# Keys laid out column by column: the spread of block-diagonal operands in an attention and FFN kernel

## The chip, the core and the metric

The kernel runs on one core of one Trainium2 chip. Its time is the device time of one execution in microseconds. The engines are TensorE (PE, with its weight loads as PEld), VectorE (DVE), ScalarE (ACT), GpSimd (POOL) and SyncE (SP), which issues most of the DMAs.

## The reference

Two things are computed one after the other: a linear attention with a decaying state, over 4 batches, 8 heads, 768 tokens and head dimension 48, and on its output a feed-forward net with a maximum over three products.

```python
def _attn_ref(r, k, v, w, u):
    state = np.zeros((B, H, D, D))
    for t in range(S):
        kt, vt, rt = (k[:, :, t], v[:, :, t], r[:, :, t])
        cur = np.einsum('bhd,bhe->bhde', u[None] * kt, vt)
        y[:, :, t] = np.einsum('bhd,bhde->bhe', rt, state + cur)
        state = w[None, :, :, None] * state + np.einsum('bhd,bhe->bhde', kt, vt)

def _moe_ref(x, w1, w2, w3, w_out):        # x: 3072 x 384, hidden 768
    h = np.maximum(np.maximum(x @ w1, x @ w2), x @ w3)
    return h @ w_out
```

All inputs and the output are float32.

## The kernel before, in words

The 768 tokens are cut into 12 chunks c of 64 tokens. In a chunk the attention is matrix products: scores of 64 by 64 tokens (keys against receptances), masked, times the values, plus the receptances times the state of the chunks before; and the state's update, keys times values. The 32 pairs of batch and head are 16 units of two heads each, and a chunk is worked in two halves q of 8 units (U = 8). The two heads of a unit share one 128 x 128 weight array: one head's 64 rows and columns stand in the upper left block, the other's in the lower right, and the rest is zero. So a product of a unit is one matmul with a block-diagonal weight operand.

To keep the precision, a float32 operand is split into two float16 parts, high and low (`high` on ScalarE, L334; `low` on VectorE, L339 and L341), and a product is three matmuls (`three`, L411): high x high, high x low, low x high. So scores are 24 matmuls a half chunk (weights `kb`, 64 columns moving), keys for the state 24 (weights `ktb`, 48 columns moving), values 48 (weights `vb` and `sb`). The FFN (L489) runs in fp32r with the same three parts and 256 moving columns, 216 matmuls a chunk.

A block-diagonal operand is a `Block` (L308): 128 partitions and, one after the other, two parts s of 8 units of w columns; for the keys w is 128, so a partition holds 2 x 8 x 128 float16 values, 4 KB. ScalarE and VectorE write a dense tile of the same shape (`kd`, `ktd`): all 128 partitions, columns 0 to 63 of each unit (0 to 47 for ktd), zeros behind. Two DMAs (`spread`, L320) carry it into the block-diagonal one (`kb`, `ktb`): partitions 0 to 63 as they stand, with their zeros, and partitions 64 to 127 shifted by 64 columns. Each of kb, ktb, kd and ktd exists once and is used for both halves of every chunk. The weights of a matmul are a slice of 128 neighbouring columns (`on`).

Chunk 0 has no spread. ScalarE writes float32 values straight into the two diagonal blocks (`apart`, L478), in the same bytes seen as 8 units of float32 columns (`wide`), and one full-precision product a unit follows (`full`, L484), for scores, values and keys.

The order of the work is made ahead by a planner (`Plan`, L38): each step has an engine, a due time, a cost and the steps that it needs, the planner plays them through, and the result is the program order of every engine, fixed when the kernel is built. `before_scores` (L718) lines up the scaling of k, `high` and `low` into kd, the spread to kb; `before_keys` (L740) the same for the state's keys; `scored` and `keyed` the matmuls. Each spread is planned as two DMA issues on SP's queue. At the start 16 half weights of the FFN arrive as float64 words and are converted on ScalarE and VectorE (L241 to L252), while chunk 0's attention runs; from c = 3 on GpSimd takes over a part of VectorE's multiplications.

Of the kernel before, what the change touches and what calls it, by code (L numbers as in the profile page):

```python
# [7 lines left out]
F32 = mybir.dt.float32  # L8
F32R = mybir.dt.float32r
F16 = mybir.dt.float16  # L10
# [8 lines left out]
P = 128  # L19
B, H, S, D = 4, 8, 768, 48  # L20
C = 64
# [5 lines left out]
U = 8  # L27
# [10 lines left out]
class Plan:  # L38
# [26 lines left out]
    def do(self, due, eng, cost, fn, reads=(), writes=(), takes=(), size=0, near=0):  # L65


        n = len(self.todo)
        new = [t for _, t in takes]
        made = (*new, *writes, *reads)[0]  # L70
        kind = eng + " " + (made if isinstance(made, str) else made[0])
        late = due > self.OPENING
        due += self.SHIFT.get(kind, (0, 0))[late]
        need = {self.wrote[k] for k in (*reads, *writes) if k in self.wrote}
        for k in writes:
            need |= self.read.get(k, set())
# [74 lines left out]
def kernel(ctx, tc, feat, tok, wu, ut, ws, wo, cst, out):  # L151
    nc = tc.nc
    const = ctx.enter_context(tc.tile_pool(name="const", bufs=1))
    raw = ctx.enter_context(tc.tile_pool(name="raw", bufs=3))
    bd = ctx.enter_context(tc.tile_pool(name="bd", bufs=1))
# [8 lines left out]
    psa = ctx.enter_context(tc.tile_pool(name="psa", bufs=4, space=PSUM))  # L164
# [7 lines left out]
    raws = {}  # L172
# [102 lines left out]
    for g in range(NP):  # L275
        nc.vector.tensor_tensor_scan(
            out=pw[:, g, 1:C + 1], data0=w_sb[:, g:g + 1].broadcast_to([P, C]), data1=ones,
# [27 lines left out]

    class Block:  # L308


        def __init__(self, name, w):
            n = 2 * U * w
            t = bd.tile([P, n + P - w], F16, name=name)
            nc.gpsimd.memset(t.bitcast(F32), 0.0)
            self.flat, self.w = t[:, 0:n], w
            self.dense = self.flat.rearrange("p (s u n) -> p s u n", s=2, u=U)
            self.on = [[t[:, (s * U + i) * w:(s * U + i) * w + P] for i in range(U)] for s in range(2)]
            self.wide = self.flat.bitcast(F32).rearrange("p (u n) -> p u n", u=U)

    def spread(eng, dst, src, by):  # L320
        eng.dma_start(out=dst.flat[0:C], in_=src.flat[0:C])
        eng.dma_start(out=dst.flat[C:P, by:], in_=src.flat[C:P, 0:2 * U * src.w - by])

    kb = Block("kb", P)
    vb = [Block(f"vb{q}", 2 * D) for q in range(2)]
    ktb = Block("ktb", P)
    kd = Block("kd", P)
    vd = [Block(f"vd{q}", 2 * D) for q in range(2)]
    sd = Block("sd", 2 * D)
    sb = [Block(f"sb{q}", 2 * D) for q in range(2)]  # L330
    ktd = Block("ktd", P)

    def high(dense, src, w, scale=1.0):
        nc.scalar.mul(out=dense.dense[:, 0, :, 0:w], in_=src, mul=scale)  # L334

    def low(dense, src, w, scale=1.0):

        if scale == 1.0:
            nc.vector.tensor_tensor(out=dense.dense[:, 1, :, 0:w], in0=src, in1=dense.dense[:, 0, :, 0:w], op=ALU.subtract)  # L339
        else:  # L340
            nc.vector.scalar_tensor_tensor(out=dense.dense[:, 1, :, 0:w], in0=src, scalar=scale, in1=dense.dense[:, 0, :, 0:w], op0=ALU.mult, op1=ALU.subtract)  # L341
# [10 lines left out]

    def units(a):
        return a.rearrange("p g b n -> p (g b) n")

    HS = (slice(0, C), slice(C, P))

    def by_token(a, q):
        return a[:, 2 * q:2 * q + 2].unsqueeze(2).broadcast_to([P, 2, B, D])
# [5 lines left out]
    def scale(c, q, n):  # L365
        t = raws[c, q]
        tb = (wkt if n == "kT" else wrt)[:, 2 * q:2 * q + 2].unsqueeze(2).broadcast_to([P, 2, B, C])
        helper(c).tensor_tensor(out=t[n], in0=t[n], in1=tb, op=ALU.mult)  # L368

    def r_high(c, q):  # L370
        t = raws[c, q]
        t["rh"] = work.tile([P, U, C], F16, name="rh", bufs=2)
        nc.scalar.copy(out=t["rh"], in_=units(t["rT"]))

    def r_low(c, q):
        t = raws[c, q]
        t["rl"] = work.tile([P, U, C], F16, name="rl", bufs=2)
        nc.vector.tensor_tensor(out=t["rl"], in0=units(t["rT"]), in1=t["rh"], op=ALU.subtract)
# [26 lines left out]
    def decay(c, q):  # L405
        t = raws[c, q]
        helper(c).tensor_tensor(out=t["k"], in0=t["k"], in1=by_token(tkt, q), op=ALU.mult)
# [67 lines left out]
    def apart(dst, src, by, scale=1.0):  # L475

        for hh in range(2):
            nc.scalar.mul(out=dst.wide[HS[hh], :, hh * by:hh * by + src.shape[2]], in_=src[HS[hh]], mul=scale)  # L478

    def full(name, q, block, n, w, src):  # L480
        t = raws[0, q]
        ps = t[name] = psa.tile([P, U, n], F32, name="psa")
        for i in range(U):
            nc.tensor.matmul(out=ps[0:w, i, :], lhsT=block.wide[:, i, 0:w], rhs=src[:, i, :], start=True, stop=True)  # L484


    def pairs3(ps, prods, first=True, last=True):
# [89 lines left out]
    def general():  # L577
# [28 lines left out]
        with tc.For_i(0, NCH, 1) as c:  # L606
# [5 lines left out]
            for s in range(C):  # L612
                vr = xp.tile([P, NP, B, D], F32, name="xl")
                for hh in range(2):
                    row = tok[bass.ds(c, 1), :, hh * C + s:hh * C + s + 1, 2].rearrange("c q p g b e -> (c p) q g b e")
                    nc.sync.dma_start(out=vr[HS[hh]].rearrange("p (q g) b e -> p q g b e", q=2), in_=row.broadcast_to([C, 2, 2, B, D]))
                kc, rc = (t[:, :, :, s:s + 1].broadcast_to([P, NP, B, D]) for t in cols)
# [53 lines left out]
    do = plan.do  # L671
# [3 lines left out]
    def dma(due, fn, size, reads=(), writes=(), takes=(), eng="sp", n=1):  # L675
        do(due, eng, n * Plan.ISSUE[eng], fn, reads, writes, takes, size)

    def helping(c, columns):
        return ("pool", 0.05 + 2.5e-3 * columns) if c > 2 else ("dve", dve(columns))

    def dve(columns):
        return 0.07 + 1.05e-3 * columns

    def act(columns):
        return 0.11 + 0.83e-3 * columns
# [32 lines left out]
    def before_scores(c, q, due):  # L718

        h, cost = helping(c, U * C)  # L720
        f, t, u = ("feat", c, q), ("tok", c, q), units
        do(due - 0.32, h, cost, lambda: scale(c, q, "kT"), reads=[f], writes=[("kT", c, q)], near=0.55)
        do(due - 0.30, h, cost, lambda: scale(c, q, "rT"), reads=[f], writes=[("rT", c, q)], near=0.55)
        do(due - 0.26, "act", act(U * C), lambda: high(kd, u(raws[c, q]["kT"]), C), reads=[("kT", c, q)], writes=["kdh"])
        do(due - 0.24, "dve", dve(U * C), lambda: low(kd, u(raws[c, q]["kT"]), C), reads=[("kT", c, q), "kdh"], writes=["kdl"], near=1.2)
        dma(due - 0.22, lambda: spread(nc.sync, kb, kd, C), 524288, reads=["kdh", "kdl"], writes=["kb"], n=2)
        do(due - 0.15, "act", act(U * C), lambda: r_high(c, q), reads=[f, ("rT", c, q)], takes=[("rh", ("rh", c, q))])
        do(due - 0.13, "dve", dve(U * C), lambda: r_low(c, q), reads=[f, ("rT", c, q), ("rh", c, q)], takes=[("rl", ("rl", c, q))], near=1.2)
        before_mask(c, q, due)
# [10 lines left out]
    def before_keys(c, q, due):  # L740
        t = ("tok", c, q)
        h, cost = helping(c, U * D)
        do(due - 0.30, h, cost, lambda: decay(c, q), reads=[t, "tkt"], writes=[("kdec", c, q)], near=0.55)
        do(due - 0.24, "act", act(U * D), lambda: high(ktd, units(raws[c, q]["k"]), D), reads=[t, ("kdec", c, q)], writes=["ktdh"])
        do(due - 0.23, "dve", dve(U * D), lambda: low(ktd, units(raws[c, q]["k"]), D), reads=[t, ("kdec", c, q), "ktdh"], writes=["ktdl"], near=1.2)
        dma(due - 0.20, lambda: spread(nc.sync, ktb, ktd, C), 524288, reads=["ktdh", "ktdl"], writes=["ktb"], n=2)

    def before_values(c, q, due):
        t, vh, vl = ("tok", c, q), ("vdh", q), ("vdl", q)
# [19 lines left out]
    def first_keys(q, due):  # L769
        c, t = 0, ("tok", 0, q)  # L770
        do(due - 0.30, "dve", dve(U * D), lambda: decay(c, q), reads=[t, "tkt"], writes=[("kdec", c, q)], near=0.55)
        do(due - 0.24, "act", 1.05, lambda: apart(ktb, units(raws[c, q]["k"]), C), reads=[t, ("kdec", c, q)], writes=["ktb"])
        do(due, "pe", 3.2, lambda: full("ke", q, ktb, D, C + D, units(raws[c, q]["v"])), reads=["ktb", t], takes=[("psa", ("ke", c, q))])
        after_keys(c, q, due)

    def scored(c, q, due):
# [115 lines left out]
    for q in range(2):  # L892
        first_keys(q, 0.1 + 0.2 * q)
        spread_state(0, q, 0.2 + 0.2 * q)
# [82 lines left out]
```

## Time and profile before

| what | value |
|---|---|
| median of two runs | 417.5 us (415.71 and 419.3) |
| profiled execution | 417.51 us, span 415.6 us, granted clock 0.998 |
| TensorE busy | 392.5 us (94%), 4758 matmuls seen |
| VectorE, ScalarE, GpSimd busy | 285.2, 256.5, 182.4 us |
| moved by DMA | 90.08 MB, mean 217 GB/s |
| weights from kb, from ktb | 528 and 480 half-precision matmuls |
| spreads of kd, of ktd | 22 and 20, two issues each |

In the rows quoted below, `L411 PE MATMUL psa<-rh,kb 128*128 128x64 f16 x352 | 19.2, 193` means: line 411, on TensorE, writes psa from rh and kb, weights of 128 rows and columns, 64 columns moving, 352 times, busy 19.2 us, 193 ns for one. The duration of a matmul or weight load runs from its start to its modelled end; matmuls overlap, so the distance from one start to the next is much shorter than this. Behind the second bar stands the time that the engine was idle just before, with what ended it. In windows each engine has its busy time and in brackets its count.

### The profile page before, as it was taken

Reading aid. Unit: us, or ns where it says so; the run is one execution under the profiler, and the core shown is the slowest. Engines: PE = TensorE matmul, PEld = TensorE weight load, DVE = VectorE, ACT = ScalarE, POOL = GpSimd, SP = SyncE. Lnnn points to the kernel's source line nnn. Section 1 sums busy time; section 2 is a strip of 40 time slices with the busy share of each in tenths; the row PEclk is TensorE's granted clock in tenths of the full one; section 3 lists DMA queues with packets and bytes.
Section 4 is the critical chain, followed back from the end, with each engine's and each line's share of the span. In section 5 each row is a group of like instructions: output and inputs, shape, how many; then the busy total and the mean of one; then the engine's idle time right before and its main releaser. Section 6 shows DMA issues by size and latency. Waiting matters only on the chain.

```text
span 415.6 us, 11976 instructions
## 1 busy us (share of the span) xinstructions
PE 392.5 (94%) x4758; PEld 388.0 (93%) x4758; DVE 285.2 (69%) x551; ACT 256.5 (62%) x674; POOL 182.4 (44%) x180
## 2 busy tenths in 40 slices
PE   1878899999999999999999999999999999999996
PEld 0767899999999999999999999999999999999996
DVE  7798999989597776676576676576676596354240
ACT  2999977796666666466366466366366377265331
POOL 9000000088669664564654754664654551020120
PEclk9999999999999999999999999999999999999999
DMA  7789898789799896876876876876876995886101
GB/s 284 288 269 249 249 278 313 193 244 302 202 270 263 227 250 170 250 196 153 259 192 143 271 194 156 256 196 153 257 192 155 299 322 139 248 289 217 38 2 41
DMA packets 30954, 90.08 MB, mean 217 GB/s; under 512 B 4784, under 2 KB 9648, under 8 KB 30896
## 3 DMA queue, kind: packets, MB, share of 16 engines
q1 hardware_dynamic: 25568, 84.47, 70.7%
q10 hardware_dynamic: 5328, 4.82, 3.7%
q8 instruction: 38, 0.62, 0.6%
q14 instruction: 20, 0.16, 0.1%
HBM read 45.85 MB, written 4.72 MB: 122 GB/s over the span
## 4 chain that ended last, share of the span: by engine, by line
PE 72%; ACT 12%; DVE 6%; DMA 5%; issue 3%; SPq 0%; ACTq 0%; DVEq 0%
PE psm L489 60%; PE psa L411 11%; ACT junk L351 3%; DMA tok<-in_tok_dram 2%; DMA ktb<-ktd 2%; ACT ztop L241 2%; ACT am L399 1%; DVE wl L252 1%; ACT wh L248 1%; DVE m L504 1%; ACT xh L467 1%; DMA out_dram<-io 1%; DVE sc L281 1%; ACT kb L478 1%; DVE raw L245 1%
## 5 line engine op out<-in xcount | busy, mean ns | idle before, releaser
L489 PE MATMUL psm<-xh,wh 128*128 128x256 f32 x648 | 166.3, 286 | 5.0 <-ACT xh L467 2.9
L489 PE MATMUL psm<-xl,wh 128*128 128x256 f32 x648 | 163.4, 282 | 1.1 <-DVE xl L472 1.1
L489 PEld LDWEIGHTS psm<-xh,wh 128*128 128x128 f32 x648 | 123.2, 190 | 5.7 <-ACT xh L467 3.1
L489 PEld LDWEIGHTS psm<-xl,wh 128*128 128x128 f32 x648 | 122.8, 190 | 1.4 <-DVE xl L472 1.4
L489 PE MATMUL psm<-xh,wl 128*128 128x256 f32 x648 | 112.6, 283 | 0.0
L504 DVE TENSOR_TENSOR m<-psm,m 128x256 f32<-128x256 f32 x144 | 60.4, 420 | 64.7 <-PE psm L489 59.1
L489 PEld LDWEIGHTS psm<-xh,wl 128*128 128x128 f32 x648 | 92.8, 190 | 0.0
L368 POOL TENSOR_TENSOR feat<-feat,wrt 128x512 f32<-128x512 f32 x36 | 47.0, 1317 | 76.1 <-DMA feat<-in_feat_dram 75.3
L513 POOL TENSOR_TENSOR hl<-m,hh 128x256 fp32r<-128x256 f32 x55 | 45.4, 827 | 74.5 <-ACT hh L507 74.4
L507 ACT CAST hh<-m 128x256 fp32r<-128x256 f32 x72 | 28.7, 403 | 55.7 <-DVE m L504 55.2
L489 PE MATMUL psm<-hh,woh 128*128 128x256 f32 x216 | 54.3, 284 | 0.0
L489 PE MATMUL psm<-hh,wl 128*128 128x256 f32 x216 | 53.4, 279 | 0.0
L387 POOL TENSOR_TENSOR am<-tok,u_sb 128x384 f32<-128x384 f32 x18 | 21.0, 1168 | 59.2 <-DVE al L431 59.2
L351 ACT ACTIVATE junk<-tok 128x384 bf16<-128x384 f32 x72 | 37.4, 520 | 14.2 <-DMA tok<-in_tok_dram 12.4
L489 PEld LDWEIGHTS psm<-hh,woh 128*128 128x128 f32 x216 | 40.6, 188 | 0.0
L489 PEld LDWEIGHTS psm<-hh,wl 128*128 128x128 f32 x216 | 40.6, 188 | 0.0
L472 DVE SCALAR_TENSOR_TENSOR xl<-psa,xh 32x256 fp32r<-32x256 f32 (+2 forms) x60 | 28.2, 471 | 14.9 <-ACT xh L467 14.0
L489 PE MATMUL psm<-hl,woh 128*128 128x256 f32 x216 | 35.1, 280 | 0.0
L467 ACT ACTIVATE xh<-psa 32x256 fp32r<-32x256 f32 (+2 forms) x60 | 25.1, 418 | 15.8 <-PE psa L411 14.8
L411 PE MATMUL psa<-ah,vb 128*128 128x64 f16 x352 | 32.9, 194 | 0.0
L411 PE MATMUL psa<-rh,sb 128*128 128x64 f16 x352 | 32.5, 193 | 0.0
L339 DVE TENSOR_TENSOR kd<-feat,kd 128x512 f16<-128x512 f32 x22 | 18.3, 830 | 20.4 <-ACT kd L334 17.3
(99 smaller groups left out, 746.3 us busy)
## 6 DMA issues: line engine op xcount, KB each, us to landing
tok<-in_tok_dram SPq DMA_DIRECT2D x24, 576.0 KB, 6.7
raw<-in_ws_dram SPq DMA_DIRECT2D x24, 576.0 KB, 7.4
feat<-in_feat_dram SPq DMA_DIRECT2D x24, 512.0 KB, 5.2
kb<-kd SPq DMA_DIRECT2D x22, 256.0 KB, 5.7
kb<-kd SPq DMA_DIRECT2D x22, 248.0 KB, 5.8
ktb<-ktd SPq DMA_DIRECT2D x20, 256.0 KB, 3.4
ktb<-ktd SPq DMA_DIRECT2D x20, 248.0 KB, 4.2
raw<-in_wo_dram SPq DMA_DIRECT2D x8, 576.0 KB, 5.6
```

The lines of the kernel that those rows point to most:

```text
L241: nc.scalar.copy(out=ztop[h].bitcast(F16).rearrange("p (n two) -> p n two", two=2)[:, :, 1], in_=halves(raw[:, 1:], 3).bitcast(BF16))
L339: nc.vector.tensor_tensor(out=dense.dense[:, 1, :, 0:w], in0=src, in1=dense.dense[:, 0, :, 0:w], op=ALU.subtract)
L351: nc.scalar.activation(out=junk, in_=src, func=AF.Square, scale=scale, accum_out=stat[:, kind, 2 * c + q:2 * c + q + 1])
L368: helper(c).tensor_tensor(out=t[n], in0=t[n], in1=tb, op=ALU.mult)
L387: helper(c).tensor_tensor(out=w.rearrange("p (g b) d -> p g b d", g=2), in0=t["r"], in1=by_token(u_sb, q), op=ALU.mult)
L411: nc.tensor.matmul(out=ps, lhsT=l[i], rhs=rr[j], start=first and n == 0, stop=last and n == 2)
L467: nc.scalar.mul(out=hi, in_=src, mul=SC_X)
L472: nc.vector.scalar_tensor_tensor(out=lo, in0=src, scalar=SC_X, in1=hi.bitcast(F32), op0=ALU.mult, op1=ALU.subtract)
L489: nc.tensor.matmul(out=ps, lhsT=a, rhs=b, start=first and n == 0, stop=last and n == len(prods) - 1)
L504: nc.vector.tensor_tensor(out=to, in0=ps, in1=m, op=ALU.max)
L507: nc.scalar.copy(out=h[0][:, f, :], in_=m)
L513: lows_by(c, f).tensor_tensor(out=h[1][:, f, :], in0=m, in1=h[0][:, f, :].bitcast(F32), op=ALU.subtract)
```

## The change

Four tiles get a new layout: `kb` and `ktb` become `Planes`, `kd` and `ktd` become `Dense`. In both a partition holds one column after the other, and in a column the 16 float16 values of two parts and eight units, 32 bytes. Neighbouring columns of one unit are thus 32 bytes apart. `Dense` has 64 columns (2 KB a partition), `Planes` 128 (4 KB), of which the off-diagonal blocks are zeroed once at the start. A spread copies two blocks of 64 partitions by 64 columns, 2 KB a partition, still as two DMAs on SP's queue.

The weights of a matmul are now 128 columns with a step of 32 bytes. `high` and `low` write with that step, and `low` reads the high part with it. Chunk 0's float32 copies (`apart`) write 4 bytes in every 32, and its full-precision products read their weights so; the keys' product takes 128 columns instead of 112. The planner's costs, sizes and due times stay the same. `vb`, `sb`, `vd` and `sd` keep their layout.

```diff
+    class Dense:
+        def __init__(self, name):
+            self.t = bd.tile([P, C, 2, U], F16, name=name)
+            nc.gpsimd.memset(self.t.bitcast(F32), 0.0)
+            self.dense = self.t.rearrange("p n s u -> p s u n")
+
+    class Planes:
+        def __init__(self, name):
+            self.t = bd.tile([P, 2 * C, 2 * U], F16, name=name)
+            nc.gpsimd.memset(self.t.bitcast(F32), 0.0)
+            self.on = [[self.t[:, :, s * U + i] for i in range(U)] for s in range(2)]
+            self.wide = self.t.bitcast(F32)
+
+        def place(self, hh, by, n):
+            return self.wide[HS[hh], hh * C:hh * C + n].rearrange("p n u -> p u n")
+
+        def whole(self, i, n):
+            return self.wide[:, :, i]
+
+    def spread_planes(dst, src):
+        for hh in range(2):
+            nc.sync.dma_start(out=dst.t[HS[hh], HS[hh]], in_=src.t[HS[hh]].rearrange("p n s u -> p n (s u)"))
...
-    kb = Block("kb", P)
+    kb = Planes("kb")
...
-    ktb = Block("ktb", P)
-    kd = Block("kd", P)
+    ktb = Planes("ktb")
+    kd = Dense("kd")
...
-    ktd = Block("ktd", P)
+    ktd = Dense("ktd")
...
-            nc.scalar.mul(out=dst.wide[HS[hh], :, hh * by:hh * by + src.shape[2]], in_=src[HS[hh]], mul=scale)
+            nc.scalar.mul(out=dst.place(hh, by, src.shape[2]), in_=src[HS[hh]], mul=scale)
...
-            nc.tensor.matmul(out=ps[0:w, i, :], lhsT=block.wide[:, i, 0:w], rhs=src[:, i, :], start=True, stop=True)
+            nc.tensor.matmul(out=ps[0:w, i, :], lhsT=block.whole(i, w), rhs=src[:, i, :], start=True, stop=True)
...
-        dma(due - 0.22, lambda: spread(nc.sync, kb, kd, C), 524288, reads=["kdh", "kdl"], writes=["kb"], n=2)
+        dma(due - 0.22, lambda: spread_planes(kb, kd), 524288, reads=["kdh", "kdl"], writes=["kb"], n=2)
...
-        dma(due - 0.20, lambda: spread(nc.sync, ktb, ktd, C), 524288, reads=["ktdh", "ktdl"], writes=["ktb"], n=2)
+        dma(due - 0.20, lambda: spread_planes(ktb, ktd), 524288, reads=["ktdh", "ktdl"], writes=["ktb"], n=2)
...
-        do(due, "pe", 3.2, lambda: full("ke", q, ktb, D, C + D, units(raws[c, q]["v"])), reads=["ktb", t], takes=[("psa", ("ke", c, q))])
+        do(due, "pe", 3.2, lambda: full("ke", q, ktb, D, P, units(raws[c, q]["v"])), reads=["ktb", t], takes=[("psa", ("ke", c, q))])
```

More of the change, by code (lines that the diff above doesn't have):

```diff
@@ L303, in turned_back @@
             nc.scalar.mul(out=tkt[hs], in_=turned[0][hs, :, hh * C:hh * C + D], mul=SC_KT)
+    HS = (slice(0, C), slice(C, P))
     class Block:
@@ L318, in __init__, with place, whole @@
             self.wide = self.flat.bitcast(F32).rearrange("p (u n) -> p u n", u=U)
+        def place(self, hh, by, n):
+            return self.wide[HS[hh], :, hh * by:hh * by + n]
+        def whole(self, i, n):
+            return self.wide[:, i, 0:n]
+    class Dense:
[9 more added lines that the diff above has]
+            self.wide = self.t.bitcast(F32)
+        def place(self, hh, by, n):
+            return self.wide[HS[hh], hh * C:hh * C + n].rearrange("p n u -> p u n")
+        def whole(self, i, n):
+            return self.wide[:, :, i]
+    def spread_planes(dst, src):
+        for hh in range(2):
+            nc.sync.dma_start(out=dst.t[HS[hh], HS[hh]], in_=src.t[HS[hh]].rearrange("p n s u -> p n (s u)"))
     def spread(eng, dst, src, by):
@@ L354, in units @@
         return a.rearrange("p g b n -> p (g b) n")
-    HS = (slice(0, C), slice(C, P))
     def by_token(a, q):
```

## The prediction

> **What bounds the kernel now.** I read the page first, busy times and the slices, then the windows by stage, then the waits of TensorE, and last the chain of waits for the pace of the matmuls. The busy times (engine, busy us, share, instructions):
>
> ```profile
> span 415.6 us, 11976 instructions
> PE 392.5 (94%) x4758; PEld 388.0 (93%) x4758; DVE 285.2 (69%) x551; ACT 256.5 (62%) x674; POOL 182.4 (44%) x180
> DMA packets 30954, 90.08 MB, mean 217 GB/s; under 512 B 4784, under 2 KB 9648, under 8 KB 30896
> ```
>
> The windows of three stages (stretch, length, busy of PE, PEld, DVE, ACT, POOL with counts, clock, DMA share, GB/s), and TensorE's waits between 45 and 131 us and between 131 and 400 us:
>
> ```profile
> 0.00:45.00 45.00, 28.18 (x160) 26.46 (x160) 37.04 (x68) 36.06 (x85) 10.44 (x19) 1.00 0.80 263
> 45.00:131.00 86.00, 83.64 (x1111) 82.47 (x1112) 74.00 (x138) 65.85 (x176) 37.98 (x34) 1.00 0.90 262
> 131.00:400.00 269.00, 269.00 (x3391) 267.68 (x3392) 171.58 (x341) 151.74 (x408) 132.48 (x126) 1.00 0.73 206
> PE psm L489 <- ACT m L500: 1.8, 2, 1.3
> PE psa L411 <- DVE rl L378: 0.8, 1, 0.8
> PE psa L411 <- DMA ktb<-ktd: 0.2, 1, 0.2
> ```
>
> From 131 to 400 us TensorE has no gap at all. From 45 to 131 us it is idle for 86 - 83.64 = 2.36 us, though DMA stands at 0.90 there. In 391 us it waits for a spread of keys once, for 0.2 us. So what the change takes from the DMA queues is worth at most those 2.36 us, plus something in the first 45 us; what it adds to a matmul is paid in full. Before 45 us the bound is another one: ScalarE. Its longest wait between 10 and 45 us, and the row with which TensorE's steady run starts (start, us, in brackets the idle time before it):
>
> ```profile
> ACT kd L334 <- DVE feat L368: 0.6, 1, 0.6
> 45.29 0.38 PE L489 MATMUL psm<-xh,wh 128*128 128x256 f32 x1 [1.29 <-ACT m L500]
> ```
>
> So ScalarE runs almost back to back there, and TensorE's start at 45.29 us waits for it.
>
> **Part 1, the DMA.** The issues before (KB each, median us to landing):
>
> ```profile
> kb<-kd SPq DMA_DIRECT2D x22, 256.0 KB, 5.7
> kb<-kd SPq DMA_DIRECT2D x22, 248.0 KB, 5.8
> ktb<-ktd SPq DMA_DIRECT2D x20, 256.0 KB, 3.4
> ktb<-ktd SPq DMA_DIRECT2D x20, 248.0 KB, 4.2
> ```
>
> Each of the 42 spreads goes from 504 KB to 2 x 64 rows x 2 KB = 256 KB, together 42 x 248 KB = 10.4 of 90.08 MB. The count and order of issues on SP's queue stay as they are, so nothing there is moved past anything. In the third stage the whole saving is hidden: TensorE is busy 269.00 of 269. In the second, the chain of waits runs through transfers twice (start, us, piece):
>
> ```profile
> 96.80 9.10 DMA tok<-in_tok_dram
> 122.21 8.63 DMA ktb<-ktd
> ```
>
> These land sooner behind shorter spreads, but what they feed then waits for ScalarE and VectorE, the larger waits of the list. The ends are 0 and -2.36; I take -1.0, somewhat under the middle, as 0.2 us of the waits is a DMA's. The memsets of kd and ktd halve on GpSimd, for which neither TensorE nor ScalarE waits in the lists above; that is worth nothing.
>
> **Part 2, the matmuls of keys and scores.** 528 read kb, 480 read ktb; their weights' columns now lie 32 bytes apart instead of 2. No row of before has a weight load with such a step, so I need bounds. The pace is in the chain (a run of x matmuls with its length), the loads' durations in the groups:
>
> ```profile
> 208.41 0.61 PE psa L411 x24
> 210.17 0.71 PE psa L411 x24
> 210.88 11.75 PE psm L489 x99
> L411 PEld LDWEIGHTS <-kb 128*128 128x128 f16 x528 | 16.7, 98 | 1.4 <-issue 0.9
> L411 PEld LDWEIGHTS <-ktb 128*128 128x128 f16 x480 | 13.5, 96 | 0.7 <-issue 0.3
> L489 PEld LDWEIGHTS psm<-xl,wh 128*128 128x128 f32 x648 | 122.8, 190 | 1.4 <-DVE xl L472 1.4
> L568 PEld LDWEIGHTS psa<-good,ones 128*1 128x1 f32 x2 | 0.1, 80 | 0.1
> ```
>
> Keys (24 in 0.61 us) come every 25.4 ns, scores (24 in 0.71) every 29.6, the FFN's every 118.7. A load of one column lasts 80 ns, one of 128 half-precision columns 98: the columns themselves take about 18 ns, less than the pace, so they are hidden under the matmul before. The FFN's 128 columns take 190 - 80 = 110 ns, and fit under 118.7. That gives the far end: if the step makes a half-precision load as long as the FFN's, the pace becomes 110, and the cost is 528 x (110 - 29.6) + 480 x (110 - 25.4) = 42.5 + 40.6 = 83 us; no gain is possible, as the pace does not follow the load now. If the columns take twice as long, 36 ns, it is 528 x 6.4 + 480 x 10.6 = 8.5 us, or less if part of it still hides. I take 0, because the hidden load has a margin of 29.6 - 18 = 11.6 and 25.4 - 18 = 7.4 ns, and the rows with a step that exist (below) lose a third at most. For the range I keep 0 and 8.5 in the forecast's own case, and give what lies above to rivals.
>
> [...]
>
> **Part 3, ScalarE.** The copies into kb and ktb of chunk 0 (L478, 4 each) and the 42 into kd and ktd (L334) now write with a 32-byte step. The row of one of them, then the nearest of ScalarE, contiguous first:
>
> ```profile
> L478 ACT ACTIVATE ktb<-tok 64x384 f32<-64x384 f32 x4 | 2.1, 518 | 0.0
> L373 ACT CAST rh<-feat 128x512 f16<-128x512 f32 x22 | 13.5, 613 | 0.2
> L334 ACT ACTIVATE vd<-tok 128x384 f16<-128x384 f32 x22 | 11.3, 514 | 1.1 <-PE psa L411 0.7 <-ACT io L536 0.4
> L248 ACT CAST wh<-raw 128x576 fp32r<-128x576 f32 x12 | 8.6, 717 | 1.6 <-DVE raw L245 1.6
> L268 ACT ACTIVATE raw<-raw,beyond 128x576 f32<-128x576 int32 x16 | 13.3, 832 | 4.4 <-DVE raw L264 3.6 <-ACT raw L268 0.8
> ```
>
> 613 and 514 give 0.77 ns an element, so 576 contiguous ones would take 662. L248 reads with an 8-byte step, L268 reads and writes with it: the write costs 832 - 717 = 115 ns, 0.20 an element, and all of the step 832/662, a quarter. Ends: 0, and a doubled 0.77. Ahead of 45 us stand 4 copies to kb and 2 to kd (512 elements; the 2 by the windows in part 4) and 4 to ktb (384), each one for one on the path: at 0.20, 6 x 0.10 + 4 x 0.08 = 0.9 us; doubled, 6 x 0.39 + 4 x 0.30 = 3.6 us. I take 0.9, by the nearest row. After 45 us the 40 others add 40 x 0.1 = 4 us (16 if doubled) to 131 us and more of idle ScalarE: 20 of 86 and 117 of 269 are free.
>
> **Part 4, VectorE.** L339 now reads one operand and writes with the step. Its windows in the first two stages (busy us, count), then rows of groups:
>
> ```profile
> 0.00:45.00 45.00, 1.38 (x2) 1.00 0.80 263
> 45.00:131.00 86.00, 9.04 (x12) 1.00 0.90 262
> L339 DVE TENSOR_TENSOR kd<-feat,kd 128x512 f16<-128x512 f32 x22 | 18.3, 830 | 20.4 <-ACT kd L334 17.3 <-DMA sb<-sd 3.2
> L431 DVE TENSOR_TENSOR al<-am,ah 128x512 f16<-128x512 f32 x22 | 15.1, 687 | 0.2
> L252 DVE TENSOR_TENSOR wl<-raw,wh 128x576 fp32r<-128x576 f32 x12 | 9.0, 751 | 0.5 <-ACT wh L248 0.4
> ```
>
> L252 reads with an 8-byte step; 687 ns with 64 more elements at some 1.1 would be 757, and it took 751: nothing. A doubled pace costs 512 x 1.1 = 0.56 us each, and 14 of the 42 run before 131 us: at most 7.8 us, of which 86 - 74.00 = 12 us of idle VectorE in the second stage hides most. I take +0.5 and keep 0 and 4. The third stage has 97 us free on VectorE against 28 x 0.56 = 16.
>
> **Part 5, chunk 0.** Its products load full-precision weights from the new layout, and the keys' load 128 columns where it had 112 (start, us, count, wait):
>
> ```profile
> 18.72 3.68 PE L484 MATMUL psa<-feat,kb 128*128 128x64 f32 x16 [0.21 <-ACT kb L478]
> 23.08 3.19 PE L484 MATMUL psa<-tok,ktb 128*112 128x48 f32 x16 [0.69 <-issue]
> 26.08 2.79 PE L484 MATMUL psa<-am,vb 128*96 128x64 f32 x16
> 31.73 0.58 PE L489 MATMUL psm<-xh,wh 128*128 128x256 f32 x1 [2.87 <-ACT xh L467]
> ```
>
> Keys go from 3.19 to at most 3.68 us, twice, so 1.0 at most; the first lies ahead of an idle 2.87 us, so half: +0.5. The pace follows the columns (230, 199 and 174 ns for 128, 112 and 96), 1.75 ns a column, so here a slower column load would show at once: doubled, 64 x 128 x 1.75 = 14 us, of which the idle of 2.87 and 1.3 us and ScalarE's own queue hide some 5, leaving 9. I take 0, as for part 2.
>
> **The sum.** -1.0 + 0 + 0.9 + 0.5 + 0.5 = +0.9 us on the profiled execution, whose time is 417.51 (the span and 1.9 around it), the median of the runs too: 418.4, call it 418.5. Its own range: all gains at their ends and nothing else, 417.5 - 2.4 = 415.1, less the 1.8 us that the runs of before lie under their median, 413.5; above, 3.6 + 0.5 + 4 at once, 425.
>
> **The rivals.** First, slower: the weight load of kb and ktb comes out from under the matmul. It decides from the point where its columns take over 25 to 30 ns. At two to three times 18 (36 to 54 ns), the cost is 8.5 to 528 x 24.4 + 480 x 28.6 = 26.6 us: 427 to 445. For it: each column now is far from the next, ScalarE's rows lose with only 8 bytes between, and TensorE has no slack. Against it: the margin of 7 to 12 ns. 0.22.
>
> [...]
>
> Second: the load loses all its speed and goes column by column like the FFN's, 110 ns: 418.4 + 83 = 501 us. For it: the FFN's row shows such a load exists on this engine; against: the operand's type and its 128 columns are as before. 0.15.
>
> Third: only the opening suffers, ScalarE doubled and chunk 0's loads too: 417.5 - 1 + 3.6 + 0.5 + 0.5 + 9 = 430, or 426 without half of the loads. For it: ScalarE's 36 us there have no gap; against: the row with 0.20 ns. 0.07.
>
> Fourth: over 2% faster, under 409.2. It needs 8.3 us; after 45 us only 2.36 are there, and the spreads begin late in the opening (first and last start behind the durations):
>
> ```profile
> L321 SPq DMA_DIRECT2D kb<-kd x22: 461/467/1502, 28.9 to 350.3; - x22
> ```
>
> So the 6 us that are missing would have to come out of 16 us, in which two or three of them run. 0.02.
>
> Fifth: the change doesn't do what it says, and a spread is cut into pieces of 32 bytes, 42 x 8192 of them. The second queue's packets of some 900 bytes (5328 for 4.82 MB) took 3.7% of 16 engines' span, 46 ns each:
>
> ```profile
> q10 hardware_dynamic: 5328, 4.82, 3.7%
> ```
>
> 344,000 such would take 1.0 ms of 16 engines. Each row's 64 columns of 32 bytes are one run of 2 KB on both sides, so 0.02.
>
> **How the numbers follow.** The forecast's chance is what is left, 0.52, its time 418.5, its own range 413.5 to 425. To hold 8 in 10 the range takes in the first and third rival: 413.5 to 445, leaving the second, fourth and fifth. 2% (8.3 us, about what a measurement of this kernel can tell from no change) reaches from 409.2 to 425.9: of the rivals' 0.46 on the slow side some 0.02 falls short of 425.9, and 0.01 of the forecast's case goes to faster. Faster 0.03, within 0.53, slower 0.44.
>
> **What would show it.** Right: the groups of loads from kb and ktb stay near 98 ns, the chain's runs of 24 at 0.61 and 0.71 us, TensorE without gaps from 131 us, bytes down to about 79.7 MB, L334 on kd near 0.73 us, L339 not over 0.9. Wrong: runs of 24 that last 0.9 to 1.3 us (first rival) or over 2.5 us (second); TensorE's steady run starting well after 46 us (third); packets in the hundred thousands (fifth).

## The result, and the profile after

The changed kernel takes 494.49 us (median of two runs, 494.04 and 494.94) against 417.5: 1.182 times, with a 95% interval of 1.178 to 1.186. The forecast was 418.5 us in a range of 413.5 to 445; both were missed. From the page of the changed kernel (busy us, share, instructions; then the DMA's totals):

```profile
span 493.2 us, 11976 instructions
PE 444.7 (90%) x4758; PEld 436.1 (88%) x4758; DVE 346.2 (70%) x551; ACT 322.0 (65%) x674; POOL 189.9 (39%) x180
DMA packets 30954, 79.41 MB, mean 161 GB/s; under 512 B 4784, under 2 KB 9648, under 8 KB 30896
```

The count of instructions is the same and the DMA moves 10.7 MB less, as the change says, but three engines are busier: TensorE by 52 us, VectorE by 61, ScalarE by 66. And TensorE, which had no gap from 131 us on, has some now. The windows of the same stages:

```profile
45.00:131.00 86.00, 73.78 (x773) 72.00 (x773) 68.26 (x109) 63.99 (x137) 21.80 (x18) 0.92 0.61 181
131.00:400.00 269.00, 256.46 (x2938) 252.27 (x2938) 198.65 (x283) 174.90 (x356) 139.57 (x124) 0.99 0.51 142
```

By 131 us 773 matmuls are seen in the second stage instead of 1111, and in the third 2938 instead of 3391. The groups that changed (L370 and L375 are L334 and L339 of before, L512 is L478, L445 is L411):

```profile
L375 DVE TENSOR_TENSOR kd<-feat,kd 128x512 f16<-128x512 f32 x22 | 56.3, 2557 | 35.9 <-ACT kd L370 35.9
L370 ACT ACTIVATE kd<-feat 128x512 f16<-128x512 f32 x22 | 53.8, 2447 | 3.4 <-ACT io L570 2.8 <-DVE feat L402 0.6
L375 DVE TENSOR_TENSOR ktd<-tok,ktd 128x384 f16<-128x384 f32 x20 | 44.5, 2224 | 8.3 <-ACT ktd L370 8.3
L370 ACT ACTIVATE ktd<-tok 128x384 f16<-128x384 f32 x20 | 38.8, 1939 | 2.9 <-POOL am L421 2.4
L445 PEld LDWEIGHTS <-kb 128*128 128x128 f16 x528 | 35.0, 162 | 1.2 <-issue 0.6
L445 PEld LDWEIGHTS <-ktb 128*128 128x128 f16 x480 | 31.6, 164 | 0.4
L512 ACT ACTIVATE kb<-feat 64x512 f32<-64x512 f32 x4 | 4.5, 1133 | 0.0
```

ScalarE's write of kd went from 630 to 2447 ns, VectorE's from 830 to 2557, the weight loads from 98 and 96 to 162 and 164. VectorE stands idle for 35.9 us ahead of its write of kd, waiting for ScalarE's; before it was 17.3. The chain of waits shows the pace of the matmuls and, in the steady stretch, where it leaves TensorE (start, us, piece; `...` stands for pieces left out):

```profile
286.79 2.39 ACT kd L370
...
289.44 1.33 PE psm L523 x9
290.76 1.42 PE psa L445 x48
292.18 1.24 PE psm L523 x9
293.42 1.52 PE psa L445 x24
294.94 1.15 PE psm L523 x9
296.08 1.53 PE psa L445 x24
297.62 7.52 PE psm L523 x63
...
308.66 2.48 ACT kd L370
```

Keys and scores take 1.52 to 1.53 us for 24, so some 63.4 ns each instead of 25.4 and 29.6; values, whose weights kept their layout, stay at 1.42 for 48. And twice in a chunk the chain leaves TensorE and runs through a write of kd. Keys of one chunk start at 256.31 and of the next at 293.42 us: a chunk lasts 37.1 us instead of 31.2 (208.41 to 239.63 before).

### The profile page after: what moved, and what is told of

Its sections match the earlier page's. It is cut to its first block, busy times and chain, and to the rows that moved or that the text cites. A ratio compares the mean times of both kernels' runs of the same rounds, so it can differ in the third digit from the quotient of the medians.

```text
span 493.2 us, 11976 instructions
## 1 busy us (share of the span) xinstructions
PE 444.7 (90%) x4758; PEld 436.1 (88%) x4758; DVE 346.2 (70%) x551; ACT 322.0 (65%) x674; POOL 189.9 (39%) x180
## 2 busy tenths in 40 slices
DMA packets 30954, 79.41 MB, mean 161 GB/s; under 512 B 4784, under 2 KB 9648, under 8 KB 30896
## 4 chain that ended last, share of the span: by engine, by line
PE 46%; ACT 16%; issue 6%; DVE 4%; ACTq 1%; DMA 1%; DVEq 0%; SPq 0%
PE psm L523 34%; PE psa L445 12%; ACT kd L370 6%; ACT ktd L370 2%; ACT junk L387 2%; DVE m L538 2%; ACT io L570 2%; ACT xh L501 1%; ACTq L909 1%; DMA sb<-sd 1%; ACT ah L460 1%; DVE kd L375 1%; ACT m L534 1%; ACT vd L370 1%; ACT rh L407 1%
## 5 line engine op out<-in xcount | busy, mean ns | idle before, releaser
L523 PE MATMUL psm<-xh,wh 128*128 128x256 f32 x648 | 171.3, 293 | 20.7 <-ACT m L534 9.3
L523 PE MATMUL psm<-xl,wh 128*128 128x256 f32 x648 | 166.4, 286 | 1.1 <-DVE xl L506 1.1
L523 PEld LDWEIGHTS psm<-xh,wh 128*128 128x128 f32 x648 | 126.0, 194 | 24.7 <-ACT m L534 10.7
L402 POOL TENSOR_TENSOR feat<-feat,wrt 128x512 f32<-128x512 f32 x36 | 50.5, 1413 | 89.9 <-DMA feat<-in_feat_dram 88.7
L375 DVE TENSOR_TENSOR kd<-feat,kd 128x512 f16<-128x512 f32 x22 | 56.3, 2557 | 35.9 <-ACT kd L370 35.9
L370 ACT ACTIVATE kd<-feat 128x512 f16<-128x512 f32 x22 | 53.8, 2447 | 3.4 <-ACT io L570 2.8
L375 DVE TENSOR_TENSOR ktd<-tok,ktd 128x384 f16<-128x384 f32 x20 | 44.5, 2224 | 8.3 <-ACT ktd L370 8.3
L387 ACT ACTIVATE junk<-tok 128x384 bf16<-128x384 f32 x72 | 41.7, 580 | 3.0 <-ACT io L570 1.3
L370 ACT ACTIVATE ktd<-tok 128x384 f16<-128x384 f32 x20 | 38.8, 1939 | 2.9 <-POOL am L421 2.4
L445 PE MATMUL psa<-al,vb 128*128 128x64 f16 x176 | 32.2, 197 | 7.3 <-DVE al L465 7.3
L534 ACT COPY m<-psm 128x256 f32<-128x256 f32 x72 | 30.0, 419 | 11.9 <-PE psm L523 10.8
```

Source lines behind the costliest of these rows:

```text
L387: nc.scalar.activation(out=junk, in_=src, func=AF.Square, scale=scale, accum_out=stat[:, kind, 2 * c + q:2 * c + q + 1])
L445: nc.tensor.matmul(out=ps, lhsT=l[i], rhs=rr[j], start=first and n == 0, stop=last and n == 2)
L523: nc.tensor.matmul(out=ps, lhsT=a, rhs=b, start=first and n == 0, stop=last and n == len(prods) - 1)
L534: nc.scalar.copy(out=m, in_=ps)
```

## The experiments

Two things could have cost the 77 us: the loads, at 528 x 33.8 + 480 x 38.0 = 36 us of TensorE, and the writes. The first four runs undo them one by one. In all of them the bytes that are moved stay the same; the products are then of other numbers.

**Loads packed, writes stepped.** `on` takes 128 neighbouring values:

```diff
-            self.on = [[self.t[:, :, s * U + i] for i in range(U)] for s in range(2)]
+            flat = self.t.rearrange("p n k -> p (n k)")
+            self.on = [[flat[:, (s * U + i) * P:(s * U + i + 1) * P] for i in range(U)] for s in range(2)]
```

> The changed kernel, but the half-precision matmuls take 128 neighbouring values of kb and ktb as weights (the same bytes in another order, so the products are other numbers; a few scales are smaller to keep them finite, and the final range test is made to pass). ScalarE's and VectorE's writes keep their 32-byte step. Theory A (two separate costs: slow loads, 528 x 33.8 + 480 x 38 = 36 us of TensorE, and slow writes behind the other 41): pace back to 29.6 and 25.4 ns, time 494.5 - 36 = 458 us. Theory B (the writes on ScalarE and VectorE set the period of 37.2 us a chunk, the loads only fill its gaps): 485 to 494 us, TensorE with more idle time. Theory C (nothing but the loads): 418 us.

Measured: 484.46 us, ratio 1.157 (1.151 to 1.163). The loads are back at 99 (kb) and 96 ns (ktb), and only 10 of the 77 us are gone; that is theory B, and the time lies just under its range. The chunk lasts 36.8 us (keys from 364.72 to 401.49 in its chain) with TensorE waiting more:

```profile
131.00:400.00 269.00, 242.43 (x2995) 236.39 (x2994) 201.15 (x287) 175.96 (x357) 142.06 (x124) 0.96 0.54 151
```

**Writes packed, loads stepped.**

```diff
-            self.dense = self.t.rearrange("p n s u -> p s u n")
+            self.dense = self.t.rearrange("p n s u -> p (n s u)").rearrange("p (s u n) -> p s u n", s=2, u=U)
```

> The changed kernel, but ScalarE and VectorE write kd and ktd unit after unit, 64 neighbouring values each, into the same 2 KB a partition (the bytes then stand in another order, so the products are other numbers; one scale is smaller, and the final range test is made to pass). Weights keep their 32-byte step. Theory A: L370 on kd back to 0.63 us, L375 to 0.69, pace of keys and scores stays at 63.4 ns, time 417.5 + 36 + 2 for the opening = 455 us. Theory B: about 455 too, but e1 then does not fall. Theory D (the loads are slow because they meet the stepped writes in the memory): pace back to 30 ns, time 420 us.

Measured: 454.16 us, ratio 1.087 (1.082 to 1.092). The pace stays at 1.52 us for 24, so the loads are slow by themselves and not by meeting the writes (theory D falls). TensorE is busy without a gap again, and the chunk is just its work: keys start at 330.62 and 365.26 us in the chain, 34.6 us, and 31.2 + 48 x 0.0338 + 48 x 0.038 = 34.7.

```profile
131.00:400.00 269.00, 269.00 (x3178) 267.70 (x3177) 156.88 (x306) 141.88 (x379) 134.98 (x125) 1.00 0.57 165
```

**Both packed, and the spread alone.** The third run has both edits. The fourth also gives chunk 0 two tiles of its own in the old layout (the keys' product is changed in the same way):

```diff
+    kb0 = Block("kb0", P)
+    ktb0 = Block("ktb0", P)
...
-        do(due - 0.29, "act", 1.25, lambda: apart(kb, units(raws[c, q]["kT"]), C), reads=[("kT", c, q)], writes=["kb"])
+        do(due - 0.29, "act", 1.25, lambda: apart(kb0, units(raws[c, q]["kT"]), C), reads=[("kT", c, q)], writes=["kb"])
...
-        do(due, "pe", 3.65, lambda: full("sc", q, kb, C, P, units(raws[c, q]["rT"])), reads=[f, "kb", ("rT", c, q)], takes=[("psa", ("sc", c, q))])
+        do(due, "pe", 3.65, lambda: full("sc", q, kb0, C, P, units(raws[c, q]["rT"])), reads=[f, "kb", ("rT", c, q)], takes=[("psa", ("sc", c, q))])
```

> Both at once: weights and the writes to kd and ktd packed, the spreads of 256 KB and chunk 0's float32 layout as in the changed kernel (again other numbers, range test made to pass). Left of the change are the shorter spreads and chunk 0's stepped copies and loads. Theory A: before plus the opening, 417.5 - 1 + 3 = 419.5 us. If a cost is still hidden in the spreads: over 425.

> As the run with both packed, and chunk 0 has its own two tiles in the old layout (two memsets more on GpSimd, behind the others; keys' product of 112 columns again). Left of the change is only that a spread moves 256 KB instead of 504. All theories: 415 to 417.5 us, between all and nothing of the 2.36 us that TensorE idled between 45 and 131 us; the difference to the run before it is the price of chunk 0's steps, 1 to 4 us.

Measured: 420.82 us, ratio 1.006 (1.003 to 1.009), and 416.65 us, ratio 0.998 (0.995 to 1.001). So what the shorter spreads alone are worth cannot be told from nothing (-2.3 to +0.3 us), and chunk 0's stepped copies and loads cost the 4.2 us between the two. The chunk of the third run lasts 31.2 us (306.19 to 337.41), as before the change.

These four runs are one table of time: both packed 421, loads stepped 454, writes stepped 484, both 494. The costs, 33 and 64 us, do not add: in the steady stretch the chunk lasts 31.2, 34.6, 36.8 and 37.1 us, near the longer of the two. The loads' extra time mostly fills gaps that the writes leave on TensorE.

**What the step costs.** Where ScalarE and VectorE walk in the order of memory, eight neighbouring values are written one after the other, and the input is read with a step:

```diff
+        if isinstance(dense, Dense):
+            nc.scalar.mul(out=dense.t[:, 0:w, 0, :], in_=src.rearrange("p u n -> p n u"), mul=scale)
+            return
```

(`low` likewise.)

> The changed kernel with its layout and full result, but ScalarE and VectorE go through kd and ktd in the order of memory: eight neighbouring float16 values of a column (16 bytes) are written one after the other, and the float32 input is read with a step of 256 (kd) or 192 bytes (ktd) instead. Weights keep the 32-byte step. Theory W (the price is in the stepped 2-byte writes): L370 on kd 0.63 to 1.1 us, L375 0.7 to 1.2, time as with packed writes, 454 to 458 us. Theory X (any walk that leaves the line with each element costs, reads too): kd stays at 1.1 to 2.4 us on ScalarE, time 460 to 494 us.

Measured: 455.42 us, ratio 1.095 (1.090 to 1.099), on the level of the run with packed writes. The walk in the order of memory, reading with a step of 256 bytes and writing eight values at a time, costs too, but far less than writing 2 bytes with a step of 32:

```profile
L371 ACT ACTIVATE kd<-feat 128x512 f16<-128x512 f32 x22 | 25.1, 1143 | 3.5 <-ACT io L576 2.9 <-DVE feat L408 0.6
L379 DVE TENSOR_TENSOR kd<-feat,kd 128x512 f16<-128x512 f32 x22 | 27.2, 1234 | 18.3 <-ACT kd L371 18.3
```

So theory W holds for most of the price; of theory X the 1.1 us stay. Two runs change the steps; e is the number of values in a column, 8 for kb and 4 for ktb in the first, 2 and 32 in the second (the writes of kd and ktd are changed in the same way, and the 32 has a tile of its own, both not shown):

```diff
+                by = flat.rearrange("p (g n e) -> p g e n", n=P, e=e)
+                self.on = [[by[:, (s * U + i) // e, (s * U + i) % e] for i in range(U)] for s in range(2)]
```

> For durations only, the products are other numbers and the final range test is made to pass. Weights from kb with a step of 16 bytes, from ktb of 8; ScalarE and VectorE write kd with 16 and ktd with 8. Theory L (the cost is lines of 16 bytes: a step of 16 pays in full, 8 half or nothing): pace of scores 63 ns, of keys 25 to 32; L370 on kd 2.4 us, on ktd 0.6 to 1.1. Theory S (the cost grows with the step): scores 30 to 45 ns, keys 25 to 30, kd 1.2 to 1.7 us, ktd 0.7 to 0.9.

> For durations only, as the run before it. Weights from kb with a step of 4 bytes, from ktb of 64 (a tile of zeros of 16 KB a partition... the spread goes to its old place); kd is written with a step of 4 bytes, ktd packed. Theory L: scores 29.6 ns, keys 63 (64 bytes as 32), kd 0.6 to 0.7 us. Theory S: keys over 100 ns, kd 0.7 us.

(The far tile is 8 KB a partition.) The two took 467.86 and 435.70 us, one run each. Their loads, first steps of 16 (kb) and 8 bytes (ktb), then 4 (kb) and 64 (ktbfar):

```profile
L477 PEld LDWEIGHTS <-kb 128*128 128x128 f16 x528 | 33.9, 167 | 1.5 <-issue 0.9
L477 PEld LDWEIGHTS <-ktb 128*128 128x128 f16 x480 | 17.6, 118 | 0.4
```

```profile
L477 PEld LDWEIGHTS <-ktbfar 128*128 128x128 f16 x480 | 31.1, 168 | 0.4
L477 PEld LDWEIGHTS <-kb 128*128 128x128 f16 x528 | 17.0, 99 | 0.6
```

The pace in their chains (24 matmuls): 0.72 us with 4 bytes, 0.82 with 8, 1.48 with 16, 1.53 with 64. ScalarE's write of kd takes 792 ns with 4 bytes and 2549 with 16, that of ktd 1122 with 8 (630 and 523 packed):

| step of the weights, bytes | 2 | 4 | 8 | 16 | 32 | 64 |
|---|---|---|---|---|---|---|
| ns between matmuls | 25.4 keys, 29.6 scores | 30.0 scores | 34.2 keys | 61.7 scores | 63.4 both | 63.8 keys |

Loads and 2-byte writes grow up to a step of 16 bytes and hardly further: a load lasts 98 and 96 ns packed, 99 with a step of 4, 118 with 8, 167 with 16, 162 and 164 with 32 and 168 with 64, and ScalarE's write of kd 2549 ns with 16 and 2447 with 32. These are the times of theory L, though with a step of 8 keys and ktd lie just past the upper ends that it gave: ScalarE's write has doubled there (523 to 1122 ns) and the keys lose 9 ns each. The lines that theory L speaks of were an assumption: the rows show the step and its price, and no run shows what lies behind it.

**The spread by pieces.** Packed weights and writes in a kernel with the full result: kd of 2 KB, the zeros left out by pieces of 128 bytes, chunk 0 in its own tiles. Of the edit, the spread:

```diff
-            nc.sync.dma_start(out=dst.t[HS[hh], HS[hh]], in_=src.t[HS[hh]].rearrange("p n s u -> p n (s u)"))
+            nc.sync.dma_start(out=dst.flat.rearrange("p (k n) -> p k n", n=P)[HS[hh], :, HS[hh]], in_=src.t[HS[hh]].rearrange("p s u n -> p (s u) n"))
```

> A kernel with the full result: weights, writes and chunk 0 packed as before the change, and a spread without zeros by pieces of 64 values (128 bytes), 1024 pieces a DMA, from a compact kd of 2 KB a partition; chunk 0 has its own two tiles. Theory: packets rise by 42 x 2 x 1024 = 86,000; at the 46 ns of the small packets of before they take 42 x 2048 x 46 / 16 = 247 us of 16 engines, 5.9 us a spread, where the 4 KB packets of before took 1.5; DMA share near 1.0, time 420 to 460 us. If packets of 128 bytes inside the core are as cheap by the byte as long ones: 416 to 418 us.

Measured: 416.09 us, ratio 0.999 (0.996 to 1.001). The packets are there (111,594 instead of 30,954), but the first queue's share of the engines is what it was before the change:

```profile
q1 hardware_dynamic: 106208, 73.81, 70.9%
```

70.9% against 70.7 with 84.47 MB: the bytes saved are given back by the packets. In the run with the spread alone, with the same bytes in packets of 2 KB, the share is 61.1%; so 80,640 packets more take 0.709 x 415.4 - 0.611 x 413.3 = 42 us of 16 engines, some 8 ns more for each, where I expected 46 for a packet. The kernel cannot be told from before.

**Why the writes cost 64 us.** ScalarE and VectorE had 117 and 97 us free in the third stage, so the busy time alone does not explain it. Two runs step one engine only, each engine with a tile of its own (VectorE with both its read and its write), and a third VectorE's read alone; `far` is the stepped view of a tile, `near` the packed one, and the lines shown are those of the first:

```diff
+            nc.scalar.mul(out=dense.far[0][:, 0, :, 0:w], in_=src, mul=scale)
...
+                nc.vector.tensor_tensor(out=dense.near[1][:, 1, :, 0:w], in0=src, in1=dense.near[0][:, 0, :, 0:w], op=ALU.subtract)
```

> As the run with packed loads (other numbers, range test made to pass), but only ScalarE writes with the 32-byte step; VectorE reads and writes packed, its half in a second tile of the same size, and a spread takes one half from each tile. Theory P (TensorE can run ahead of ScalarE and VectorE only by its four PSUM tiles, some 3 to 4 us; ScalarE's 2.4 us and VectorE's wait for it and its own 2.4 us add up past that, one alone hardly does): 425 to 440 us. Theory Q (each microsecond on ScalarE or VectorE costs a like part): half of the 66 us, 445 to 455.

> The reverse: ScalarE writes packed, VectorE reads the high part and writes the low with the 32-byte step, loads packed. Theory P: 425 to 440 us. Theory Q: 445 to 455 us. L375 on kd 2.4 us in both.

> Only VectorE's read of the high part has the 32-byte step; its write, ScalarE's write and the loads are packed. Theory W (writes cost): L375 on kd stays at 0.69 us, 420 us. Theory X (reads cost too): 1.2 to 2.4 us.

Measured: 447.16 us, ratio 1.072 (1.068 to 1.075), with ScalarE's step; 441.76, ratio 1.059 (1.055 to 1.063), with VectorE's; 427.17 (one run) with VectorE's read alone, where L384 on kd takes 1438 ns. Above the 421 of the packed run that is 26, 21 and 6 us. Theory P's range was missed by both. Theory Q's takes in the first time and not the second, and the 26 + 21 = 47 lie under the 64 of both together, so a like part for each microsecond does not hold either. (In the second, VectorE's write of kd was also longer than expected, 3.0 us in the median.) What happens in a stretch with both shows on VectorE of the changed kernel (start, us, in brackets the wait):

```profile
307.33 0.95 DVE L538 TENSOR_TENSOR m<-psm,m 128x256 f32<-128x256 f32 x2 [0.74 <-ACT m L534]
311.16 2.90 DVE L375 TENSOR_TENSOR kd<-feat,kd 128x512 f16<-128x512 f32 x1 [2.88 <-ACT kd L370]
313.68 1.16 DVE L538 TENSOR_TENSOR m<-psm,m 128x256 f32<-128x256 f32 x2
```

From 308.3 to 313.7 us VectorE empties no PSUM: 2.9 us of waiting for ScalarE and 2.5 of its own write. As an estimate from the FFN's pace before (118.7 ns), TensorE could go on with the FFN's matmuls alone for four PSUM tiles of 9, 4 x 1.07 = 4.3 us. Here it does not stop at once, for values, keys and scores come in between in its order; the delay goes on through ScalarE, which waits for VectorE in turn (start, us, wait; the last line is from the chain):

```profile
314.87 0.41 ACT L541 CAST hh<-m 128x256 fp32r<-128x256 f32 x1 [3.53 <-DVE m L538]
...
320.92 1.90 ACT L370 ACTIVATE ktd<-tok 128x384 f16<-128x384 f32 x1 [0.49 <-POOL am L421]
...
323.95 2.40 ACT L370 ACTIVATE kd<-feat 128x512 f16<-128x512 f32 x1 [0.47 <-ACT io L570]
325.88 0.68 ACT L534 COPY m<-psm 128x256 f32<-128x256 f32 x1
326.62 1.33 PE psm L523 x9
```

ScalarE loses 3.5 us, writes ktd and kd, and only then copies m out of PSUM; TensorE, 1.4 us idle by then, starts behind this copy. To test whether it is the room in PSUM, I first gave two products one buffer, to have room for eight:

```diff
...
+            if not spare:
+                two = psm.tile([P, 2, n], F32, name="psm")
+                spare.extend([two[:, 1], two[:, 0]])
+            ps = spare.pop()
```

> The run with packed loads and stepped writes (484 us), with the same order on every engine, but two of the FFN's first products share one 2 KB PSUM buffer, so that TensorE can be up to eight products of 9 matmuls ahead of ScalarE and VectorE (8 x 1.07 = 8.6 us) instead of four (4.3 us). Other numbers, range test made to pass. Theory P (the stepped writes cost because ScalarE's write, VectorE's wait for it and VectorE's own 2.4 us, 5.4 us in a row, hold up the emptying of PSUM for longer than TensorE can run ahead): the stalls go for the most part, 425 to 450 us. Rival R (the longer writes lengthen the chain from k to the scores and the state, which no buffer shortens): 475 to 485 us.

Measured: 507.82 us, ratio 1.217 (1.211 to 1.223): slower, which no theory said. TensorE waits 40.8 us for VectorE, 8 times up to 6.2; whether two products that share a buffer wait for each other's emptying was not taken apart, so the run does not tell. The three that followed do. In the first VectorE does not wait for ScalarE, because it subtracts its own old output; in the others the FFN has three tiles instead of four:

```diff
-            nc.vector.tensor_tensor(out=dense.dense[:, 1, :, 0:w], in0=src, in1=dense.dense[:, 0, :, 0:w], op=ALU.subtract)
+            nc.vector.tensor_tensor(out=dense.dense[:, 1, :, 0:w], in0=src, in1=dense.dense[:, 1 if isinstance(dense, Dense) else 0, :, 0:w], op=ALU.subtract)
```

```diff
-    psm = ctx.enter_context(tc.tile_pool(name="psm", bufs=4, space=PSUM))
+    psm = ctx.enter_context(tc.tile_pool(name="psm", bufs=3, space=PSUM))
```

> The run with packed loads and stepped writes (484 us), but VectorE's low part subtracts its own old output (the same step and size) instead of ScalarE's fresh high part, so that it no longer waits for ScalarE. Other numbers, range test made to pass. Theory P (TensorE stalls because ScalarE's 2.4 us and VectorE's 2.4 us stand one behind the other on VectorE, which empties no PSUM meanwhile): the two now overlap, 440 to 460 us, not far over the runs with one of them stepped (447 and 442). Theory R (the long writes cost by their own length, one after the other or not): 475 to 485 us.

> The run with packed loads and stepped writes (484 us) with three PSUM tiles for the FFN instead of four; same order on every engine, other numbers. Theory P: TensorE can run ahead by 3.2 instead of 4.3 us, each pair of long writes costs about 1 us more, 42 x 1 us at most: 500 to 525 us. Theory R: no more than the same step costs with packed writes, below.

> The run with packed loads and packed writes (421 us) with three PSUM tiles instead of four: what a tile less costs where no instruction is long. Theory P: 421 to 432 us, clearly less than the tile costs with stepped writes. Theory R: the same difference as there.

Measured: without the wait 447.97 us, ratio 1.074 (1.067 to 1.080); three tiles 510.23, ratio 1.222 (1.218 to 1.227), with stepped writes, and 427.98, ratio 1.026 (1.023 to 1.029), with packed ones. The writes are no shorter in the first of them, and VectorE's wait ahead of its own is gone:

```profile
L376 DVE TENSOR_TENSOR kd<-feat,kd 128x512 f16<-128x512 f32 x22 | 61.1, 2776 | 0.0
L371 ACT ACTIVATE kd<-feat 128x512 f16<-128x512 f32 x22 | 53.4, 2427 | 3.4 <-ACT io L571 2.8 <-DVE feat L403 0.6
```

Taking away the wait between the two writes gives back 36 of the 64 us with both still stepped. A PSUM tile less costs 26 us with the long writes and 7 without. What TensorE waited for in the run with packed loads and stepped writes (us, times, longest) says the same:

```profile
PE psm L524 <- ACT m L535: 10.8, 8, 1.7
PE psm L524 <- ACT io L571: 10.2, 7, 2.7
PE psm L524 <- DVE m L539: 8.5, 9, 2.6
```

These 29.5 us are waits for ScalarE and VectorE to empty PSUM; with packed writes they are 1.0. No wait of TensorE in either run ends on a spread. Its waits for parts of the attention that ScalarE and VectorE make (al, ah, rh, rl) grow too, from 1.3 to 10.7 us; whether a longer chain (theory R of the run with eight tiles) or the same queues cause these was not taken apart, but they are the smaller part. So theory P holds in kind: the writes cost because they stand one behind the other in the order of two engines that must empty PSUM, and the emptying falls behind by more than TensorE can run ahead. The numbers that theory P gave for one engine were too low by 2 to 7 us at the upper end; what one long write costs was not taken apart.

The traces also say how the 64 us lie on TensorE. Between these two runs its idle time grows by 39 us (from 23.7 to 63.0) and its busy time by 25 (from 396.1 to 420.8) with the same matmuls, at a mean granted clock of 0.956 against 0.999. As an estimate, this clock alone would make 414 us of the 396.1.

## Why the prediction was wrong, point by point

**What bounds the kernel** was read rightly: TensorE without a gap, 2.36 us at most to be had from the DMA. **Part 1** (-1.0 us, between 0 and -2.36) is compatible with the spread alone, 416.65 against 418.6 us of the kernel before measured beside it, an interval of -2.3 to +0.3 that takes in zero as well.

**Part 2** failed at "I take 0, because the hidden load has a margin". The weights of kb and ktb load in 162 and 164 ns, the pace is 63.4, and the cost, 36 us of TensorE (33 measured alone), lies between the first rival's 26.6 and the second's 83. The point from which it decides, columns of over 25 to 30 ns, fits the rows: 99 - 80 = 19 ns with a step of 4 bytes cost nothing, 118 - 80 = 38 ns with 8 cost 9. With 32 bytes the columns take 162 - 80 = 82 ns, of which 63 come through in the pace. So runs of 24 last 1.52 us, between the signs of the first rival (0.9 to 1.3) and of the second (over 2.5). The outer ends, 0 and 83 us, held; the forecast's own 0 to 8.5 did not. The choice was wrong, since the nearest rows had no step at all on TensorE. The stepped load's 162 ns are still shorter than the FFN's 190, and a step of 4 bytes is all but free (30.0 ns against 29.6), but from 8 bytes on the step is not free by any row here (34.2 ns against 25.4 with 8, 61.7 against 29.6 with 16). The rows with a step that I leaned on were of other engines, such as ScalarE's L268, which lost a quarter (832 against 662 ns) with a step of 8 bytes.

**Part 3** failed by size and by reasoning. The price of 0.20 ns an element came from a 4-byte write with an 8-byte step; a 2-byte write with 32 costs (2447 - 630)/512 = 3.5, past the upper end of 0.77. Chunk 0's 4-byte copies went from 626 to 1133 and from 518 to 907 ns, 1.0 an element, so 4 x 0.51 + 4 x 0.39 = 3.6 us where the upper end gave them 2.8; with the loads they cost 4.2 us where 0.9 + 0.5 was taken. And setting the 40 others off against "131 us and more of idle ScalarE" was the step that hid the largest loss, the 64 us of the writes: 117 free microseconds in the third stage were no cover for single instructions of 2.4 with VectorE waiting behind them.

**Part 4** failed the same way: VectorE's write went to 2.56 us where the end was 0.69 + 0.56, and its "12 us of idle VectorE in the second stage hides most" left out that VectorE waits in order for ScalarE's write, 35.9 us in all for kd. **Part 5** took 0 for chunk 0's loads; a product of 16 went from 3.68 to 4.07 us, 0.4 us more, far from the doubled pace.

**The rivals.** The second one's time, 501 us, is near the 494 measured, but that is luck: the loads keep a pace of 63 ns and not its 110, and the rest came from writes that no rival had in the steady stretch. The first had the right mechanism for 33 us. The third had the writes, but only in the opening. The fifth was rightly small; by the run with pieces packets of 128 bytes are far cheaper (some 8 ns more each) than its 46 ns, and 32 bytes were not tried.

## What to carry to other kernels

A layout that saves a transfer is paid by the engines that read and write it (here 52 us more busy on TensorE, 61 on VectorE, 66 on ScalarE): price each of them by the step between the values that it touches and not by the elements alone, with a row of the same engine, element size and step (on ScalarE a 2-byte write and a 4-byte one, both with a step of 32 bytes, differed by over three times, 3.5 and 1.0 ns more an element). Look first which engine has no slack, here TensorE, and how many instructions of it read the new layout. And free time of an engine need not cover a longer instruction if another waits for what is queued behind it (here 117 us were free on ScalarE in the third stage, and the writes cost 64): follow what waits for what from one engine to the next, and compare the delay that PSUM's emptying gathers with the room that the buffers give, not the sums of busy time.

## What the runs showed of the hardware that was not expected

- A half-precision weight load of 128 columns with 64 columns moving holds a pace of 29.6 ns with a step of 2 bytes and 30.0 with 4; with 48 moving it is 25.4 with 2 and 34.2 with 8; with 16 bytes it is 61.7 (64 moving), with 32 63.4 (both) and with 64 63.8 (48 moving). Between 16 and 64 bytes the distance hardly counted.
- A 2-byte write with a step of 32 bytes costs 3.5 ns an element more on ScalarE ((2447 - 630)/512), a 4-byte one with the same step 1.0 ((1133 - 626)/512). A 4-byte read with 256 bytes, its 2-byte values written eight at a time, also costs 1.0 ((1143 - 630)/512); reading and writing were not told apart there. Why 2 bytes cost over three times 4 was not tried.
- TensorE's granted clock was lower in stretches where it has gaps: 0.92 between 45 and 131 us of the changed kernel, and down to 0.83 in one window of it, where the kernel before has 1.00. In the run with three tiles and stepped writes the mean is 0.936. Gaps alone do not decide it: with ScalarE's step alone TensorE is idle for 10.6 us of the third stage at a clock of 1.00.

```profile
120.00:140.00 20.00, 17.32 (x179) 17.13 (x179) 12.43 (x18) 12.91 (x30) 8.75 (x8) 0.83 0.53 147
```

- Inside the core, 86,016 packets of 128 bytes (42 x 2 x 1024) in place of the spreads' 5,376 of some 4 KB (42 x 2 x 64) cost no time that could be measured: the first queue's share of the DMA engines was 70.9% against 70.7, with 10.7 MB less to move.
